# Downsampled probabilities and values as float16 pairs, and one rank per operation, in a fused attention and gated-MLP kernel

## The chip, the cores and the metric

One core of a Trainium2 chip. The metric is device time in microseconds of one execution; lower is better. Engines: PE (TensorE), DVE (VectorE), ACT (ScalarE), POOL (GpSimd), SP (SyncE, which issues most transfers).

## The reference

Attention of 8 batches x 8 heads, 576 positions, 64 numbers a head, feeds a gated MLP. The attention is the sum of two branches: one on queries, keys and values averaged over groups of 4 positions (144 groups), its output repeated 4 times; one on the full positions with a band mask of 3 on either side.

```python
# Attention, per head; sm_attn is softmax(q k^T / 8) v
q_d, k_d, v_d = (a.reshape(B, H, 144, 4, 64).mean(axis=3) for a in (q, k, v))
out_up = np.repeat(sm_attn(q_d, k_d, v_d), 4, axis=2)
out_local = sm_attn(q, k, v) with scores where |i - j| >= 4 set to -1e9
x = (out_up + out_local) as [batch, 576, 512]
# gated MLP
h = np.maximum(x @ w_in, 0.0)
u, v = h[..., :512], h[..., 512:]
v_n = (v - mean(v)) / sqrt(var(v) + 1e-6)
v_s = einsum('ts,bsd->btd', w_spatial, v_n) + b_spatial
out = (u * v_s) @ w_out
```

## The kernel before, in words

**Pieces.** The work is cut into pieces, each an operation of one engine with its inputs, outputs and buffers (`plan.op`). Two heads make a pair, so there are 4 pairs a batch and 32 in all, numbered n. A pair's attention: sums over groups of 4 (`sum1`, `sum2`), banded scores on PE (S, L694, forty f32 matmul records of 64x64; the mask is added by DVE, or by four mask products on PE, L687, for pairs marked T in `ON`), downsampled scores (Sd, L741), softmax steps on DVE, ACT and POOL, f32 transposes of the probabilities on PE (T, L770, banded; Td, L804, downsampled), copies to SBUF by ACT, and two value products on PE (AV, L837, banded; AVd, L827, downsampled). The sum of both goes to `x`; from batch 1 on it is split into an f16 hi part (ACT) and an f16 lo part (DVE, L865).

A batch's gated MLP: V pieces (L899 to L908), U pieces (L965, L970), spatial pieces SP (L992 to L995: 14 matmuls) and output pieces O (L1029: 12 matmuls). Batch 0 uses f32 weights straight away (f32 V and U pieces); from batch 1 on every product is three f16 products, hi x hi, hi x lo, lo x hi. The weights come as 64-bit words which DVE and ACT turn into f32 and then into f16 pairs in the opening (`low`, `shrink`, `body`, `sign`, `whi`, `wlo`; L473 to L488, L446, L449). The scale of each split comes from a bound: a transpose (L416), a maximum (L419), a product with ones (`spread`, L422) and five small DVE steps.

**Td and AVd before.** `normal_d` multiplies the 3 x 144 exponentials in `ed` by the inverse sums, in f32. `turn_d` (L804) transposes them in six f32 products with an identity, 72 keys at a time, into two PSUM banks; ACT copies each (`copy_d`, L808). `values_d` (L827) multiplies them by the downsampled f32 values `tv` in four f32 products: two column halves (heads) times two blocks of 72 keys.

**Order.** Before anything is emitted, `plan.run` (L143 to L244) lists the pieces: for each engine it takes, among those that could start within `NEAR` ns of the first, the one of the smallest rank, with `STAY` off for PE pieces in the array's present mode, and goes by assumed durations. The result is a fixed order in each engine's queue. Ranks are the pair's number plus a number for the kind of piece, from the tables `RANK` (attention), `MRANK` (gated MLP), `WRANK` and `SRANK` (weights). While PE would idle before 110 us of the plan, products on constants are put in (`warm`, L1080). `ON` says which engine does a step for the n-th pair (A ACT, D DVE, P POOL).

Of the kernel before, what the change touches and what calls it, by code (L numbers as in the profile page):

```python
# [76 lines left out]
class Plan:  # L77
# [14 lines left out]
    def buf(self, tag):  # L92
        b = Buf(tag, self.count[tag])
        self.count[tag] += 1
        return b

    def op(self, eng, ns, fn, r=(), w=(), hold=(), after=(), rank=0.0, lag=None, port=False, kb=0, mode="",
           name=""):
# [25 lines left out]
        for t in (*r, *w, *hold):  # L124
            b = t if isinstance(t, Buf) else t[0] if isinstance(t, tuple) else None
            if isinstance(b, Buf) and b not in o.bufs:
                o.bufs.append(b)
                b.left += 1
# [3 lines left out]
    def run(self, near=150.0, stay=0.0, dma=(1500.0, 4.2, 500.0), emit=True):  # L132
# [6 lines left out]
        since = {t: [0.0] * len(v) for t, v in self.places.items()}  # L139
        end = 0.0  # L140
# [108 lines left out]
RANK = {"load": [-94.58, 127.99, 43.89, 60.21, -107.64, 28.27, -122.54, 3.37, -146.09, 126.37],  # L249
        "vload": [183.17, 159.9, -72.4],  # L250
        "vabs": [15.5, 92.34, -30.01],
        "tv": [14.64, -124.04, -101.65],
        "sum": [65.95, 32.66, 176.64, 185.55, 155.19, 82.2, 190.54, 200, 174.16, 200],
# [22 lines left out]
SRANK = {"WV": [-14.84, -71.59, -150.09, -200],
        "WU": [-144.08, 40.42, -170.35, -167.93],
        "WSP": [-187.21, -48.19, -200, -172.6, -159.59],
        "WO": [-94.51, 19.4, -185.76, 42.74]}
NEAR = 101  # L280
STAY = 24.8
# [8 lines left out]
ON = {"shrink": "AAAADA",  # L290
      "sum": "DPDPDPPDPDDDDPDDPD",
      "mask": "DDDTTTDTDTDDDDDDTDDDDTD",
      "norm": "PPPDPPDPDDDPPDDDDPDDPPPPDPPPDP",
      "normd": "DPPPPPDDPPAPPAAPPPPDPDPPDDAPDAD",
      "vlo": "DPDDDPPDPDDDDPDDDPPDPPDDDDPPPDPPDPDDDPD"}
# [3 lines left out]
def tile_kernel(ctx, tc, qk, vw, v4, w_in, wT, bsp, w_out, out, emit=True):  # L299
# [58 lines left out]
    places("g", 2, [P, NF, 2, HA[1]], F16)  # L358
# [4 lines left out]
    places("gt", 1, [P, NF, 2, 2 * TAIL], F16)  # L363
# [5 lines left out]
    places("tv", 2, [72, NP, 4 * D], F32)  # L369
# [9 lines left out]
    places("pdT", 1, [72, 2, 3, 96], F32)  # L379
# [17 lines left out]
    places("wst", NT + 1, [P, S], F32)  # L397
# [200 lines left out]
    x_of, tail_of, tv_of, sx_of, v_of, gt_of, og_of = {}, {}, {}, {}, {}, {}, {}  # L598
# [42 lines left out]
    def attention(n):  # L641
# [484 lines left out]
```

## Time and profile before

| | |
|---|---|
| median of 3 runs | 580.74 us (578.71 to 585.12) |
| profiled execution | 581.14 us |
| its span, first to last instruction | 579.3 us |
| mean granted TensorE clock | 0.979 of full |
| PE busy | 555.9 us |
| DVE, ACT, POOL busy | 427.9, 333.6, 142.0 us |

The span is what the trace covers; the profiled execution is 1.8 us longer. Busy time of PE counts a matmul from its start to its modelled end, so neighbours overlap; the chain of waits counts from start to start.

### The profile page before, as it was taken

Reading aid. Unit: us, or ns where it says so; the run is one execution under the profiler, and the core shown is the slowest. Engines: PE = TensorE matmul, PEld = TensorE weight load, DVE = VectorE, ACT = ScalarE, POOL = GpSimd, SP = SyncE. Lnnn points to the kernel's source line nnn. Section 1 sums busy time; section 2 is a strip of 40 time slices with the busy share of each in tenths; the row PEclk is TensorE's granted clock in tenths of the full one; section 3 lists DMA queues with packets and bytes.
Section 4 is the critical chain, followed back from the end, with each engine's and each line's share of the span. In section 5 each row is a group of like instructions: output and inputs, shape, how many; then the busy total and the mean of one; then the engine's idle time right before and its main releaser. Section 6 shows DMA issues by size and latency. Waiting matters only on the chain.

```text
span 579.3 us, 15196 instructions
## 1 busy us (share of the span) xinstructions
PE 555.9 (96%) x6159; PEld 374.3 (65%) x6159; DVE 427.9 (74%) x1129; ACT 333.6 (58%) x901; POOL 142.0 (25%) x157
## 2 busy tenths in 40 slices
PE   5769899999999999999999999999999999999997
PEld 2456357776677666776668656775777666675573
DVE  6999996985887588884979497888768776636250
ACT  4676676665774568454665476555755555534322
POOL 3533343002422125001610163102511051002100
PEclk9876999999999999999999999999999999999999
DMA  9997634023550344323542145324431101010102
GB/s 266 282 296 219 181 72 125 30 65 108 129 116 1 119 106 107 101 84 103 108 116 70 37 105 124 102 84 105 107 101 61 60 1 40 19 37 0 40 16 91
DMA packets 37386, 56.98 MB, mean 98 GB/s; under 512 B 3651, under 2 KB 24131, under 8 KB 37317
## 3 DMA queue, kind: packets, MB, share of 16 engines
q1 hardware_dynamic: 35012, 48.94, 27.3%
q0 software_dynamic: 2304, 7.08, 7.5%
q8 instruction: 48, 0.79, 0.6%
q14 instruction: 22, 0.17, 0.1%
HBM read 46.57 MB, written 9.44 MB: 97 GB/s over the span
## 4 chain that ended last, share of the span: by engine, by line
PE 84%; DVE 9%; issue 4%; ACT 2%; POOL 1%; ACTq 0%; POOLq 0%; DVEq 0%
PE pmb L1029 5%; PE pmc L992 5%; PE pmb L992 5%; PE pma L903 5%; PE pmd L1029 4%; PE pma L992 4%; PE pmc L970 4%; PE pma L1029 4%; PE pmd L992 3%; PE pmb L970 3%; PE pma L970 3%; PE pmd L903 3%; PE pmc L903 3%; PE pmd L970 3%; PE pmc L1029 2%
## 5 line engine op out<-in xcount | busy, mean ns | idle before, releaser
L992 PEld LDWEIGHTS <-vha 128*128 128x128 f16 x768 | 73.8, 98 | 21.1 <-issue 2.6
L970 PEld LDWEIGHTS <-win 128*128 128x128 f16 x672 | 65.0, 98 | 19.4 <-issue 2.7
L762 POOL TENSOR_TENSOR sa<-sa,sma 128x640 f32<-128x640 f32 x12 | 17.3, 1440 | 110.1 <-DVE sma L729 71.9
L1029 PEld LDWEIGHTS <-gb 128*128 128x128 f16 x192 | 18.6, 98 | 20.4 <-issue 0.2
L1029 PEld LDWEIGHTS <-ga 128*128 128x128 f16 x192 | 18.4, 98 | 20.2 <-issue 0.2
L992 PE MATMUL pmc<-wsp,vha 128*128 128x256 f16 (+1 forms) x216 | 29.2, 284 | 0.0
L992 PE MATMUL pmb<-wsp,vha 128*128 128x256 f16 (+1 forms) x216 | 28.8, 283 | 0.0
L992 PE MATMUL pma<-wsp,vha 128*128 128x320 f16 (+1 forms) x180 | 24.7, 286 | 0.0
L792 POOL TENSOR_TENSOR eda<-eda,smda 128x432 f32<-128x432 f32 x8 | 8.9, 1113 | 60.7 <-DVE smda L783 30.6
L707 DVE TENSOR_TENSOR sa<-paa,mask 128x384 f32<-128x384 f32 (+1 forms) x16 | 7.1, 486 | 21.9 <-PE paa L694 21.9
L992 PE MATMUL pmd<-wsp,vha 128*128 128x320 f16 (+1 forms) x156 | 22.1, 291 | 0.0
L934 POOL TENSOR_TENSOR stc<-stc,mhalf 128x1 f32<-128x1 f32 (+1 forms) x13 | 9.7, 744 | 49.6 <-DVE stc L915 49.6
L762 POOL TENSOR_TENSOR sb<-sb,smb 128x640 f32<-128x640 f32 x7 | 9.9, 1421 | 39.9 <-ACT gb L1002 26.6
L934 POOL TENSOR_TENSOR sta<-sta,mhalf 128x1 f32<-128x1 f32 (+1 forms) x14 | 11.4, 813 | 29.0 <-DVE sta L915 29.0
L934 POOL TENSOR_TENSOR stb<-stb,mhalf 128x1 f32<-128x1 f32 (+1 forms) x13 | 11.6, 894 | 20.9 <-DVE stb L915 20.9
L1029 PE MATMUL pmb<-wo,ga 128*128 128x512 f16 x72 | 16.6, 379 | 0.0
L1029 PE MATMUL pma<-wo,gb 128*128 128x512 f16 x72 | 16.5, 379 | 0.0
L758 ACT ACTIVATE sa<-sa 128x640 f32<-128x640 f32 x16 | 11.8, 739 | 5.7 <-DVE sw L427 3.0
L903 PEld LDWEIGHTS <-xa 128*128 128x128 f16 x84 | 8.2, 98 | 9.9
L610 POOL DMA_DIRECT2D tva<-v_dram x12 | 11.2, 932 | 13.6 <-DMA tva<-v_dram 13.6
L778 ACT ACTIVATE eda<-pmc,mxda 128x144 f32<-128x144 f32 x19 | 7.1, 377 | 11.9 <-DVE mxda L746 10.0
L1029 PE MATMUL pmd<-wo,ga 128*128 128x512 f16 x60 | 13.8, 379 | 0.0
(1034 smaller groups left out, 1692.5 us busy)
## 6 DMA issues: line engine op xcount, KB each, us to landing
qka<-qk_dram SPq DMA_DIRECT2D x16, 576.0 KB, 4.3
qkb<-qk_dram SPq DMA_DIRECT2D x16, 576.0 KB, 5.3
tva<-v_dram POOLq DMA_DIRECT2D x12, 288.0 KB, 4.9
tvb<-v_dram POOLq DMA_DIRECT2D x12, 288.0 KB, 4.4
stg<-w_in_dram SPq DMA_DIRECT2D x5, 512.0 KB, 5.1
out_dram<-rowa SPq DMA_DIRECT2D x8, 256.0 KB, 2.0
out_dram<-rowc SPq DMA_DIRECT2D x7, 256.0 KB, 4.3
more<-w_in_dram SPq DMA_DIRECT2D x3, 512.0 KB
```

What stands on the lines that cost most here:

```text
L610: plan.op("POOL", 850, lambda r=r: nc.gpsimd.dma_start(t.ap, v4[b, r], accum_op=ALU.add), w=[t], rank=rank + 2.0 + 0.3 * r, kb=288, name="tv")
L707: nc.vector.tensor_tensor(sv, pv, mask[:, None, None, :].broadcast_to(list(pv.shape)), op=ALU.add)
L758: exp_of.append(plan.op("ACT", 643, lambda: nc.scalar.activation(s.ap, s.ap, AF.Exp, scale=1.0 / 8.0), w=[s], rank=R["E"], name="exp"))
L762: plan.op(nm, 0, lambda: side(nm).tensor_tensor(s.ap, s.ap, sm.ap[:, :, None].broadcast_to([P, NW, 64]), op=ALU.mult), r=[sm], w=[s], rank ...
L778: nc.scalar.activation(ed.ap[:, a, :], down(a), AF.Exp, bias=mxd.ap[:, a:a + 1], scale=1.0 / 128.0, accum_out=smd.ap[:, a:a + 1])
L792: side(nd).tensor_tensor(ed.ap, ed.ap, smd.ap[:, :, None].broadcast_to([P, 3, G]), op=ALU.mult)
L903: nc.tensor.matmul(ps.ap, xs[c].ap[:, i, t * P:(t + 1) * P], win[:, c, j, FF:], start=(c == 0 and (i, j) == (0, 0)), stop=(c == NC - 1 and ...
L934: plan.op("POOL", 830, lambda: nc.gpsimd.tensor_tensor(st.ap[:r, 8:9], st.ap[:r, 8:9], mhalf[:r], op=ALU.pow), w=[st], rank=rank - EVICT, ...
L970: nc.tensor.matmul(ps.ap[:, :n], win[:, c, i, ft * P:(ft + 1) * P], xs[c].ap[:, j, HA[h]:HA[h + 1]], start=(c == 0 and (i, j) == (0, 0)), ...
L992: nc.tensor.matmul(ps.ap[:, :n], vh.ap[:, c, i, fs], wsp[:, c, j, hs], start=(c == 0 and (i, j) == (0, 0)), stop=False)
L1029: nc.tensor.matmul(ps.ap, g.ap[:, c, i, k:k + P] if t < NT else gt.ap[:, c, i], wo[:, c, j, :], start=(c == 0 and (i, j) == (0, 0)), stop= ...
```

## The change

1. **AVd and Td in f16, from batch 1 on.** The downsampled values `tv` are scaled and split into an f16 hi (ACT) and lo (DVE, L807, two instructions of 512 columns a batch), and four SP transfers (`move`, L813) lay them out as 96 rows of `th`. The normalized probabilities are written as f16 hi into `eh` (`normal_d`), and three new DVE instructions of 144 columns a pair write the lo part (`rest_d`, L978). Nine f16 transposes (L1011) replace six f32 ones and one bank the two; one ACT copy of 864 columns replaces two of 288. Ten f16 products (L1049) replace four f32 ones. The copy of the result (`dn`) is scaled. Batch 0 keeps the f32 forms (now L995 and L1040).
2. **Ranks.** A table `ORDER` gives every operation its rank by its number in the program, and overrides the ranks that the calls pass on. `NEAR` and `STAY` change.
3. **Engines.** `ON` is rewritten: among pairs, masks by PE (T) rise from 7 to 11; some sums, normalizing steps and lo parts change sides, and ACT takes 16 normalizing steps of the downsampled branch where it had 5.
4. **Memory.** First slots of `tv`, `th` and `eh` lie in the staging of the spatial weights `wst`, those of `g` and `gt` in the staging of w_in; `kept` holds them back until that staging is released. Two f16 identities are made by POOL at the start.

```diff
+        o.rank = ORDER[len(self.ops)]
         self.ops.append(o)
...
+ORDER = [
+    37.60, -174.26, -1122.41, -103.57, -12.79, -6.00, -3.24, -1114.52, -2299.76, -1110.97, -18.29, -668.02, -984.84, -2316.33, -1043.76,
...
-NEAR = 101
-STAY = 24.8
+NEAR = 131.8
+STAY = 5.08
...
-      "mask": "DDDTTTDTDTDDDDDDTDDDDTD",
+      "mask": "DDDTTTDTDDTTDTDDDDTTDTDDDDDDTD",
...
+        plan.op("ACT", 1000, lambda: nc.scalar.activation(both(tx, 0), tv.ap.rearrange("p j (k d) -> p j k d", k=2), AF.Copy, scale=sx.ap[:72, 10:11]),
+                r=[tv, sx.sub(10)], w=[tx.sub(0)], rank=rank, name="thi")
+
+        def low():
+            x = tv.ap.rearrange("p j (k d) -> p j k d", k=2)
+            for k in range(2):
+                nc.vector.scalar_tensor_tensor(tx.ap[:, 2 + k], x[:, :, k], sx.ap[:72, 10:11], tx.ap[:, k], op0=ALU.mult, op1=ALU.subtract)
...
+        def spread_rows():
+            a, z = th.ap[:, ::2], tx.ap
+            for dst, src in ((a[:72], z[:, ::2]), (a[72:], z[:24, 1::2]), (th.ap[0:96:2, 1::2], z[24:, 1::2]), (th.ap[1:96:2, 1::2], z[24:, 1::2])):
+                nc.sync.dma_start(dst, src)
...
+        def rest_d():
+            for a in range(3):
+                nc.vector.scalar_tensor_tensor(eh.ap[:, a, :, 1], ed.ap[:, a, :], smd.ap[:, a:a + 1], eh.ap[:, a, :, 0], op0=ALU.mult, op1=ALU.subtract)
...
+        def turn_h():
+            v = turned(ptd[0])[:96, :9 * 112].rearrange("p (c a q) -> p c a q", c=3, a=3)
+            for c in range(3):
+                for a in range(3):
+                    x = eh.ap[:112, a, 96:].rearrange("p k x -> p (k x)") if c == 1 else eh.ap[:112, a, :96, c // 2]
+                    nc.tensor.matmul(v[:, c, a], x, cross16 if a == 2 else ident16, start=True, stop=True, is_transpose=True)
...
+        def values_h():
+            t = half_t().rearrange("p (c a h q) -> p c a h q", c=3, a=3, h=2)
+            w = th_of[b].ap
+            passes = ((0, 0), (2, 0), (0, 2), (1, 1), (1, 3))
+            for i, (c, k) in enumerate(passes):
+                for h in range(2):
+                    nc.tensor.matmul(pw.ap[h * 64:h * 64 + 64, :G], w[:, k, p, h * D:h * D + D], t[:, c, :, h, :],
+                                     start=i == 0, stop=i == len(passes) - 1)
```

What stands on PE ahead of the first spatial piece, before (L687 and L694 banded scores with the mask by PE, L416 and L422 bounds, L804 Td, then L992, the spatial piece):

```order
L694 MATMUL paa<-qkb 64x64 x20
L694 MATMUL pab<-qka 64x64 x20
L416 MATMUL pma<-ident,uta 8x128
L416 MATMUL pmd<-ident,sw 4x128
L804 MATMUL pmb<-ident,eda 72x112 x2
L804 MATMUL pmb<-cross,eda 72x112
L804 MATMUL pmc<-ident,eda 72x112 x2
L804 MATMUL pmc<-cross,eda 72x112
L422 LDWEIGHTS one
L422 MATMUL pma<-uta,one 128x1
```

The same place now, from the banded scores on (L873; L1049 is pair 4's new AVd, ten loads and ten products, of which the last are shown; L575 the product with ones; L1011 the next pair's new Td, its first of nine):

```order
L1049 LDWEIGHTS th_126
L1049 MATMUL pma<-pdTa,th_126 64x144
L1049 LDWEIGHTS th_126
L1049 MATMUL pma<-pdTa,th_126 64x144
L575 LDWEIGHTS one
L575 MATMUL pmc<-uta,one 128x1
L1011 LDWEIGHTS wst
L1011 MATMUL pmb<-ident_86,wst 96x112
```

Pair 4's AVd has moved ahead of the first spatial piece (before, it followed it), and reads `th`, which four SP transfers fill.

DVE at the end of the opening, before (L940 a lo part of V, L473 to L488 conversion of w_out, L918 a normalizing step, L668 group sums, L707 mask, L419 the maximum that opens the spatial pieces):

```order
L940 TENSOR_TENSOR vha<-rowd,vha 128x512
L473 TENSOR_SCALAR mbc<-more 128x512
L473 TENSOR_SCALAR mbd<-stg 128x512
L918 TENSOR_SCALAR rowb<-rowb,stb 64x512
L484 SCALAR_TENSOR_TENSOR mbc<-rowe,mbc 128x512
L484 SCALAR_TENSOR_TENSOR mbd<-rowa,mbd 128x512
L488 SCALAR_TENSOR_TENSOR mbc<-rowe,mbc 128x512
L488 SCALAR_TENSOR_TENSOR mbd<-rowa,mbd 128x512
L668 TENSOR_TENSOR kdb<-suma 128x288
L707 TENSOR_TENSOR sb<-pab,mask 128x2x3x64
L707 TENSOR_TENSOR sb<-pab,mask 128x2x2x64
L419 TENSOR_REDUCE uta<-pma 8x1
```

And now (L807 the new lo part of the downsampled values; L1144, L1166, L847, L886 and L572 are L918, L940, L668, L707 and L419 of before; L961 and L962 the inverse of a sum):

```order
L807 SCALAR_TENSOR_TENSOR txa<-wst,sxa,txa 72x512 x2
L1144 TENSOR_SCALAR rowc<-rowc,stb 64x512
L1166 TENSOR_TENSOR vha<-rowd,vha 128x512
L572 TENSOR_REDUCE sw<-pmd 4x1
L847 TENSOR_TENSOR kdb<-suma 128x288
L961 TENSOR_SCALAR smda<-smda 128x3
L962 RECIPROCAL smda<-smda 128x3
L886 TENSOR_TENSOR sa<-pab,mask 128x2x3x64
L886 TENSOR_TENSOR sa<-pab,mask 128x2x2x64
L572 TENSOR_REDUCE uta<-pmc 8x1
```

The conversions of w_out now stand earlier, and the lo part of the values (L807) lies ahead of the maximum, with eight other instructions between.

## Rows read from the trace of the kernel before

**Rows 1.** The page: span, busy time of each engine with its share, and PE and its granted clock (tenths) in 40 equal slices.

```profile
span 579.3 us, 15196 instructions
PE 555.9 (96%) x6159; PEld 374.3 (65%) x6159; DVE 427.9 (74%) x1129; ACT 333.6 (58%) x901; POOL 142.0 (25%) x157
PE   5769899999999999999999999999999999999997
PEclk9876999999999999999999999999999999999999
```

**Rows 2.** Busy time by stretch: from and to (us), length, then each engine's busy us and instructions, granted clock, DMA share, GB/s.

```profile
0.00:54.00 54.00, 38.58 (x598) 25.73 (x598) 45.77 (x104) 31.94 (x88) 20.79 (x36) 0.81 0.93 270
54.00:70.00 16.00, 13.54 (x44) 5.86 (x44) 15.72 (x37) 10.86 (x26) 4.95 (x6) 1.00 0.72 208
70.00:98.00 28.00, 27.52 (x182) 17.64 (x182) 22.93 (x62) 20.07 (x51) 12.91 (x12) 0.94 0.31 61
98.00:576.00 478.00, 476.22 (x5339) 325.09 (x5338) 343.49 (x929) 270.69 (x737) 103.34 (x104) 1.00 0.28 78
```

**Rows 3.** The chain of waits, start and length in us, counted to the next piece's start.

```profile
95.14 0.26 PE paa L687 x4
95.40 0.58 PE paa L694 x40
...
101.09 0.65 PE pma L827 x8
...
103.38 1.31 PE pma L992 x12
...
106.44 1.63 PE pmd L992 x12
...
113.40 0.29 PE pmc L804 x3
113.69 0.29 PE pmd L804 x3
...
116.16 0.11 PE pma L741 x2
...
575.39 0.69 ACT rowa L1042
```

**Rows 4.** The stretch from 98 to 576 us, first the instructions of L827 alone, then those of L804 alone: PE's busy time and count, then its weight loads.

```profile
98.00:576.00 478.00, 20.10 (x224) 12.59 (x224) 1.00 0.28 78
98.00:576.00 478.00, 20.03 (x162) 16.36 (x162) 1.00 0.28 78
```

**Rows 5.** Weight loads by line: durations in ns (least/median/most), first and last start in us, rows x columns and type. L416, L804, L770 are transposes, L687 the bf16 mask, L694 and L899 ordinary f32 products.

```profile
L416 PEld LDWEIGHTS pmd<-ident,utc x2: 87/87/87, 229.7 to 422.0; 128*8 128x8 f32 x2
L804 PEld LDWEIGHTS pmc<-ident,eda x16: 112/113/116, 15.8 to 388.1; 112*72 112x72 f32 x16
L770 PEld LDWEIGHTS pab<-ident,sb x45: 139/141/142, 26.5 to 422.7; 128*128 128x128 f32 x45
L687 PEld LDWEIGHTS <-mask_a x28: 103/103/125, 31.4 to 331.5; 64*64 64x64 bf16 x28
L694 PEld LDWEIGHTS paa<-qka x320: 129/135/135, 6.1 to 426.2; 64*64 64x64 f32 x160
L899 PEld LDWEIGHTS pmb<-mbb,xb x4: 190/190/190, 54.5 to 62.7; 128*128 128x128 f32 x4
```

**Rows 6.** PE in the opening, in order of time: start, us, line, operation, tiles, shapes, count, and the idle time before it with what ended it. First V piece, a U step, first spatial piece.

```profile
53.99 1.13 PE L899 MATMUL pmb<-mba,xa 128*128 128x512 f32 x2
...
69.86 0.70 PE L965 MATMUL pmc<-xd,mbh 128*128 128x256 f32 x2 [1.78 <-DVE mbh L488]
...
98.06 1.48 PE L992 MATMUL pmb<-wsp,vha 128*128 128x256 f16 x12
```

**Rows 7.** DVE at the end of the opening, in the same form.

```profile
88.39 0.69 DVE L940 TENSOR_TENSOR vha<-rowd,vha 128x512 f16<-128x512 f32 x1 [0.44 <-ACT vha L938]
...
96.64 0.89 DVE L707 TENSOR_TENSOR sb<-pab,mask 128x384 f32<-128x384 f32 x2 [3.66 <-PE pab L694]
97.45 0.27 DVE L419 TENSOR_REDUCE uta<-pma 8x1 bf16<-8x128 f32 x1
```

**Rows 8.** Instructions grouped by line and form, count | busy us, mean ns | idle before; then two rows of transfers: an issue of two on SP in order of time, and a group of stores with KB each and us to landing.

```profile
L665 DVE TENSOR_TENSOR suma<-qka 128x576 f32<-128x576 f32 x14 | 10.7, 761 | 2.0 <-DMA qka<-qk_dram 2.0
L668 DVE TENSOR_TENSOR kda<-suma 128x288 f32<-128x288 f32 x13 | 6.7, 512 | 0.3
L865 DVE SCALAR_TENSOR_TENSOR xf<-xfa,sxa,xf 128x576 f16<-128x576 f32 x4 | 3.1, 784 | 0.0
L449 DVE SCALAR_TENSOR_TENSOR wo<-mba,sw,wo 128x512 f16<-128x512 f32 x1 | 0.7, 743 | 0.0
L808 ACT COPY pdTa<-pmb 72x288 f32<-72x288 f32 x19 | 7.5, 393 | 2.4 <-PE pmb L804 2.4
L792 POOL TENSOR_TENSOR eda<-eda,smda 128x432 f32<-128x432 f32 x8 | 8.9, 1113 | 60.7 <-DVE smda L783 30.6
...
97.54 1.29 SPq L624 DMA_DIRECT2D vd<-vw_dram  x2
...
out_dram<-rowd SPq DMA_DIRECT2D x4, 128.0 KB, 2.2
```

More of the change, by code (lines that the diff above doesn't have):

```diff
@@ L124, in op @@
         for t in (*r, *w, *hold):
+            if isinstance(t, Buf):
+                o.bufs += [x for x in self.held.get(t.tag, ()) if x not in o.bufs]
             b = t if isinstance(t, Buf) else t[0] if isinstance(t, tuple) else None
@@ L127, in op @@
                 o.bufs.append(b)
-                b.left += 1
+        for b in o.bufs:
+            b.left += 1
+        o.rank = ORDER[len(self.ops)]
         self.ops.append(o)
@@ L139, in run @@
         since = {t: [0.0] * len(v) for t, v in self.places.items()}
+        for b in (x for v in self.held.values() for x in v):
+            since[b.tag][b.slot] = None
         end = 0.0
@@ L276 @@
[L276 to L279, printed above, removed]
-NEAR = 101
-STAY = 24.8
+RANK = {"load": [-38.34, -38.34, -38.34, -38.34, 194.73, 194.73, 194.73, 194.73, -104.21, -104.21],
+        "vload": [28.68, 82.28, 98.76],
+        "vabs": [1.11, -27.85, 2.97],
+        "tv": [-60, -3.63, -131.09],
+        "th": [-60, -60, -60],
+        "sum": [-7.7, -7.7, -7.7, -7.7, 83.34, 83.34, 83.34, 83.34, 129.45, 129.45],
[7 rows of a table added]
+        "AVd": [-158.96, -158.96, -158.96, -158.96, -95.27, -95.27, -95.27, -95.27, -2.28, -2.28],
+        "AV": [192.01, 192.01, 192.01, 192.01, -47.84, -47.84, -47.84, -47.84, 10.31, 10.31],
+        "X": [-69.34, -69.34, -69.34, -69.34, -39.39, -39.39, -39.39, -39.39, 64.63, 64.63]}
@@ L800, in turn_d @@
+        ptd, pdT = [plan.buf("pm") for _ in range(2 if whole else 1)], plan.buf("pdT")
+        KEYS = (72, 72)
         def turn_d():
-            for kc in range(2):
-                v = ptd[kc].ap[:72, :384].rearrange("p (a q) -> p a q", a=3)
+            for kc, n in enumerate(KEYS):
+                v = ptd[kc].ap[:n, :384].rearrange("p (a q) -> p a q", a=3)
                 for a in range(3):
-                    nc.tensor.matmul(v[:, a, :112], ed.ap[:112, a, kc * 72:kc * 72 + 72], cross if a == 2 else ident[:112, :112],
+                    nc.tensor.matmul(v[:, a, :112], ed.ap[:112, a, kc * 72:kc * 72 + n], cross if a == 2 else ident[:112, :112],
@@ new lines, in half_t, with copy_h @@
+        def half_t():
+            return pdT.ap.rearrange("p c a q -> p (c a q)").bitcast(F16)[:, :9 * 96]
+        def copy_h():
+            nc.scalar.copy(half_t().rearrange("p (c q) -> p c q", q=96),
+                           turned(ptd[0])[:96, :9 * 112].rearrange("p (c q) -> p c q", q=112)[:, :, :96])
+        copies = [copied]
+        if whole:
+            plan.op("PE", 560, turn_d, r=[ed], w=list(ptd), hold=[pdT], rank=R["Td"], lag=PEL, mode="F", name="Td")
+            for kc in range(2):
+                copies += [plan.op("ACT", 290, lambda kc=kc: copy_d(kc), r=[ptd[kc]], w=[pdT.sub(kc)], rank=R["Td"] - EVICT, name="copyTd")]
+        else:
+            plan.op("PE", 442, turn_h, r=[eh.sub(0), eh.sub(1)], w=list(ptd), hold=[pdT], rank=R["Td"], lag=PEL, mode="F", name="Td")
+            copies += [plan.op("ACT", 790, copy_h, r=list(ptd), w=[pdT.sub(0), pdT.sub(1)], rank=R["Td"] - EVICT, name="copyTd")]
```

129 lines of the change are left out of this document (84 added, 45 removed), and 134 rows, old and new, of tables (ORDER, RANK).

## The prediction

> **What bounds the kernel now.** Read the page's busy times first: PE is busy 96% of the span, no other engine over 74% [rows 1]. A busy PE need not be a bound, so the table of stretches comes next [rows 2]. It splits the run in two. From 98 us to 576 us PE is busy for all but 1.8 us of 478, at full granted clock (1.00, the level of 2.4 GHz). Of that 1.8, 0.7 is the last copy, after PE has finished [rows 3], so PE really waits 1.1 us. Before 98 us it is another program: PE idles for 18.4 us, the clock is 0.81 of full up to 54 us, and DVE is busy 45.8 of 54 and then 15.7 of 16 us [rows 2]. So the opening belongs to loads and DVE, and from the first spatial piece, at 98.06 us [rows 6], every nanosecond that PE needs is a nanosecond of span. Third, the chain of waits prices the pieces from start to start, which the modelled ends of matmuls don't [rows 3].
>
> **Values matmul of the downsampled branch (AVd, L827).** On the chain four f32 products, recorded as eight matmuls, take 0.65 us [rows 3]. After 98 us there are 224 records, 28 pieces [rows 4]. A 64x144 f32 round with two column halves side by side takes 0.11 on the chain (L741, [rows 3]), so four rounds are 0.45 to 0.49 and first load and drain the other 0.16. For f16 I use two spatial pieces: twelve 256-column matmuls take 1.31 and twelve of 320 take 1.63, so 109 and 136 ns, 0.42 ns a column [rows 3]. 144 columns are 62 ns. The new piece has ten f16 products in five such rounds: 0.31 + 0.16 = 0.47, an estimate. One of the 28 now stands ahead of the first spatial piece, so 28 x 0.65 - 27 x 0.47 = 18.2 - 12.7 = 5.5 us go. Bounds: if the two halves don't run side by side, ten rounds are 0.62 + 0.16 = 0.78 and 27 of them cost 2.9 us more than before; if the drain shrinks too, 0.36 and 8.5 us go.
>
> **Transposes (Td, L804).** Six f32 transposes take 0.29 + 0.29 us [rows 3]; 162 records, 27 pieces, are left after 98 us [rows 4]: 15.7. Now nine f16 ones of 112 columns. Streaming costs 49 ns each by the same slope. But each loads 96 columns of weights first, and the trace has no f16 load of 96. The nearest rows: f32 loads in transposes last 87 ns for 8 columns, 113 for 72, 141 for 128, that is 0.45 ns a column; the bf16 mask's 64 columns last 103 [rows 5]. By that slope 96 columns take 43 ns of throughput, under the 49, and the load hides. Nine are 0.445; the order has 26 after the first spatial piece: 11.6, so 4.1 go. The other end: f32 loads of ordinary products last 135 ns for 64 columns and 190 for 128, 0.86 a column [rows 5]; 96 columns would be 83 ns and bind, 0.74 a piece, 26 x 0.74 = 19.2, a loss of 3.5. I take the first, because a transpose is what it is. The Trainium skill, "TensorE: Matmul & The Clock Gate", section "LDWEIGHTS (loading the stationary operand)", speaks against the change here: the load takes columns divided by 1.2 GHz, so 80 ns for 96; by it, an estimate, a piece is 0.72 and the term turns from -4.1 to +3.0. Its slope of 0.83 is the one of the ordinary f32 rows; the transposes' rows [rows 5] contradict it.
>
> **What else moves on PE.** Mask products by PE rise from 7 to 11 pairs, all four after 98 us: 4 x 0.26 = 1.0 [rows 3]. One downsampled score piece moves ahead: three rounds, 0.3. All other pieces (V, U, SP, O, S, T, AV) stand in the same numbers on both sides of the first spatial piece. Sum after it: -5.5 - 4.1 + 1.0 - 0.3 = -8.9 us.
>
> **The opening.** Two things reach the first spatial piece later. (a) DVE: ahead of the reduction that opens the spatial pieces (L419, 97.45 us) the order now has more. Six residue instructions of 144 columns are new to the trace: bounded by 0.1 and by the 576-column form's 0.78, I estimate 0.25, 1.5 in all; two low halves of the values of 512 columns at 0.74, 1.5; one more pair sum, 0.76 + 0.5; eight small ones, 1.2 [rows 7, 8]. That is 5.5 us, against 3.66 + 0.44 us of DVE idle time there [rows 7], which they fill: 1.4 later. (b) A new path: the low halves, then four SP transfers, then pair 4's values matmul, which stands on PE ahead of the spread, a Td and the first spatial piece; all three queue behind it. On DVE 2.8 us of work lie between the low halves and the reduction, so they end at 96.0; four issues at 0.65 are 2.6, landing 2.2 more by a 128 KB store [rows 8]: 100.8 at the latest, 99 if issues overlap flight. Then 0.47 + 0.1 + 0.45: the first spatial piece at 100 to 101.8, 2 to 3.7 late. For the other sign: four V pieces now stand ahead of the first U piece where three did, and PE's 1.8 us wait for the last converted weight (69.86, [rows 6]) can go. I take +2.5, the lower part of (b), bounds -1.8 to +8 (the opening's own clock, 0.81, shows what PE idle there does).
>
> **Edits costed at nothing.** After 98 us DVE gets 26 x 0.75 of residues and a few low halves, about 25 us on 343 busy of 478 [rows 2]; ACT's copy of the transposes is one of 864 columns instead of two of 288, at 393 ns each [rows 8], about 0.2 more, and more of the normalizing stands on ACT. PE's own work covers both. Its margin is the distance in PE's order from a pair's scores to its transposes: never under 6.4 us of PE work now, once 4.5, mostly 6.3 and up before; the chain between (maxima, exponential, inverse, normalizing up to 1.1 on POOL [rows 8], and now a residue of 0.75) grows by that last step. I allow 0.5 us, bounds 0 to 20 (all residues shown). POOL's normalizing now writes f16 at a stride; POOL is idle enough [rows 2]. The last five O pieces and the final copy and store are unchanged.
>
> **Sum.** The profiled execution took 581.1 us (span 579.3 and 1.8 around it). 581.1 - 8.9 + 2.5 + 0.5 = 575.2. It stood 0.4 above the median of 580.74, so the forecast is 574.8, 1.0% under; about 1% is what a measurement of this kernel can tell from none.
>
> **Rivals.**
> 1. *Weight loads bind the f16 transposes.* For it: the ordinary f32 slope; against it: the transposes' slope, both in [rows 5]. Term +3.5 instead of -4.1: 582.4. The skill's section on loads is this rival's rule. A second rule of that page ("Wait — 56ns, not 53.3ns?") gives some 62 ns of sequencer time per matmul, an estimate of 0.78 for the ten products; here forty matmul records of L694 take 0.58 us [rows 3], 15 ns each, so it doesn't bind.
> 2. *The opening eats it.* The transfers land late, PE idles into the lower clock: +8 instead of +2.5, 580.3. For it: 0.81 before 54 us [rows 2].
> 3. *Slower: the residue is late in every pair.* Place: PE in front of each f16 transpose; price: the whole new DVE step, 0.75 us, 28 times, +21 instead of +0.5: 595. It decides for slower from 12 us, 0.43 us a pair. For it: a strict order, and DVE at 80% and over of the 54 to 98 us. Against: PE lost only 1.1 us after 98 us before with the same distances.
> 4. *The opening gains.* The wait at 69.86 goes and the transfers find cover: -1.8 instead of +2.5 and no stall, 570.0.
>
> **How the numbers follow.** Forecast (572 to 577.5): 0.42, of which 0.25 lies over 1% below the median; rival 4: 0.23; rival 2: 0.12; rival 1: 0.12; rival 3: 0.11. Faster by over 1%: 0.25 + 0.23 = 0.48. Slower: 0.11 and the tail of rival 1, 0.12. Within: 0.40. Range 568.5 to 585: from 1.5 under rival 4 to 2.6 over rival 1; rival 3 and the tails stay out.
>
> **What would show it.** Right: L1011's nine transposes 0.44 to 0.46 us on the chain; L1049's ten products 0.45 to 0.5; the first L1218 at 100 to 102 us; PE waiting under 2 us after it. Wrong: L1011 spaced at 80 ns (rival 1); the first L1218 after 105 or before 98 (rivals 2, 4); PE waits at L1011 on DVE L978 of 0.4 us a pair (rival 3).

## The result and the profile after

The changed kernel took 571.78 us (median, 570.31 to 572.09) against 580.24 before: 0.984 of it, 95% interval 0.9803 to 0.9878. Two later groups of runs gave 0.9819 (0.9793 to 0.9844) and 0.9813 (0.9786 to 0.9841). So the change gains 1.6 to 1.9%, 9 to 11 us. The forecast was 574.8, a gain of 5.9; the measured median lies 0.2 us under the band that the prediction called its forecast (572 to 577.5), and inside its range.

The page, with the lines that answer to [rows 1]:

```profile
span 570.3 us, 15614 instructions
PE 547.1 (96%) x6307; PEld 368.4 (65%) x6307; DVE 449.1 (79%) x1227; ACT 358.5 (63%) x913; POOL 139.0 (24%) x162
PE   5778799999999999999999999999999999999997
PEclk9758999999999999999999999999999999999999
```

PE has 148 instructions more and 8.8 us less to do; DVE has 21 us more. PE's share of the span is the same 96%, so the bound has not moved: the program is shorter by what PE does less. The table of stretches, columns as in [rows 2], with the last stretch ending 0.6 us after PE does (before, 0.7):

```profile
0.00:54.00 54.00, 39.48 (x601) 26.35 (x602) 44.71 (x109) 34.88 (x94) 20.30 (x42) 0.78 1.00 262
54.00:70.00 16.00, 12.41 (x48) 5.77 (x46) 15.59 (x42) 11.31 (x28) 5.83 (x7) 1.00 0.88 207
70.00:98.00 28.00, 27.99 (x189) 17.70 (x185) 25.56 (x69) 21.39 (x58) 7.42 (x8) 0.94 0.41 86
98.00:567.00 469.00, 467.18 (x5479) 318.62 (x5474) 363.27 (x1012) 290.71 (x737) 105.42 (x107) 1.00 0.31 84
```

The opening is as it was: PE idles for 18.1 us of the first 98 (18.4 before), and the granted clock is 0.78 up to 54 us where it was 0.81. After it PE is busy for all but 1.8 us, though DVE now has 77% of that stretch where it had 72%. The chain of waits around the first spatial piece, and its end, as in [rows 3]:

```profile
95.98 2.42 DMA th<-txa
...
98.54 0.32 PE pma L1049 x4
98.96 0.58 PE pmb L1011 x9
99.53 1.31 PE pmd L1218 x12
...
107.57 0.43 PE pmb L1049 x10
...
114.56 0.45 PE pma L1011 x9
...
566.47 0.69 ACT rowa L1268
```

The chain starts a piece at the modelled end of the one before it; by its own start the first spatial piece comes at 99.37, and that is the time used below. L1049 (new AVd) takes 0.43 us on the chain, L1011 (new Td) 0.45. The path of the low halves is on the chain, as forecast: the transfer of `th`, the rest of pair 4's AVd, a Td, the first spatial piece. In the opening itself, as in [rows 6], the waits have changed places:

```profile
68.76 0.77 PE L949 MATMUL paa<-ident,sb 128*128 128x128 f32 x5 [3.59 <-POOL sb L941]
...
70.09 2.07 PE L1125 MATMUL pmb<-mba,xa 128*128 128x512 f32 x2
...
98.54 0.32 PE L1049 MATMUL pma<-pdTa,th 96*64 96x144 f16 x4 [0.41 <-DMA th<-txa]
```

The wait of 1.78 us for the converted weights is gone, a wait of 3.59 for POOL's normalizing stands just ahead of it, and after it a V round takes 2.07 us where the rounds before took 1.02: PE is on its lower level. It was on it at that place before, too; over 70 to 98 us the granted clock is 0.94 in both kernels. PE waits 0.41 us for the transfer. After the first spatial piece the groups of waits name two of any size (us in total, times, longest):

```profile
PE pma L1011 <- DVE eh L978: 0.4, 1, 0.4
PE pma L569 <- ACT ug L1202: 0.3, 1, 0.3
```

**Where the time came from.** I give each PE instruction the time from its start to the next one's start, and sum by kind, from the first spatial piece (L992, now L1218) to the start of PE's last instruction. These sums hold the waits, and add up to the whole stretch. The remaining kinds (spatial, O, V, T, S, AV, spreads) differ by 0.2 us at most.

| kind | before | after | difference | forecast |
|---|---|---|---|---|
| AVd | 18.20 | 11.76 | -6.4 | -5.5 |
| Td, with the waits within and right behind it | 15.82 | 13.15 | -2.7 | -4.1 |
| mask by PE | 0.48 | 1.12 | +0.6 | +1.0 |
| Sd | 10.25 | 9.73 | -0.5 | -0.3 |
| U, with a wait of 0.7 us at 288 us before | 84.14 | 83.25 | -0.9 | part of +0.5 |
| whole stretch | 476.86 | 466.64 | -10.2 | -8.4 |
| first spatial piece at | 98.06 | 99.37 | +1.3 | +2.5 |

### The profile page after: what moved, and what is told of

Read it like the earlier page. It is cut to its first block, busy times and chain, and to the rows that moved or that the text cites. A ratio compares the mean times of both kernels' runs of the same rounds, so it can differ in the third digit from the quotient of the medians.

```text
span 570.3 us, 15614 instructions
## 1 busy us (share of the span) xinstructions
PE 547.1 (96%) x6307; PEld 368.4 (65%) x6307; DVE 449.1 (79%) x1227; ACT 358.5 (63%) x913; POOL 139.0 (24%) x162
## 4 chain that ended last, share of the span: by engine, by line
PE 82%; DVE 10%; DMA 4%; ACT 2%; issue 1%; SPq 0%; POOL 0%; DVEq 0%; POOLq 0%; ACTq 0%
PE pma L1255 5%; PE pmc L1255 5%; PE pmd L1218 4%; PE pma L1196 4%; PE pma L1218 4%; PE pmb L1218 4%; PE pmc L1218 4%; PE pmb L1196 4%; PE pma L1129 4%; PE pmc L1129 4%; PE pmd L1255 3%; PE pmb L1255 3%; PE pmd L1129 3%; PE pmb L1129 3%; PE pmd L1196 3%; PE paa L1060 2%
## 5 line engine op out<-in xcount | busy, mean ns | idle before, releaser
L1218 PEld LDWEIGHTS <-vha 128*128 128x128 f16 x768 | 73.6, 98 | 19.5
L1196 PEld LDWEIGHTS <-win 128*128 128x128 f16 x672 | 64.8, 98 | 18.4
L1255 PEld LDWEIGHTS <-more 128*128 128x128 f16 x192 | 18.5, 98 | 20.8
L1255 PEld LDWEIGHTS <-g 128*128 128x128 f16 x192 | 18.3, 98 | 20.8
L1218 PE MATMUL pmd<-wsp,vha 128*128 128x320 f16 (+1 forms) x192 | 27.5, 292 | 0.0
L1218 PE MATMUL pma<-wsp,vha 128*128 128x256 f16 (+1 forms) x192 | 26.2, 286 | 0.0
L1218 PE MATMUL pmb<-wsp,vha 128*128 128x256 f16 (+1 forms) x192 | 25.5, 282 | 0.0
L1218 PE MATMUL pmc<-wsp,vha 128*128 128x256 f16 (+1 forms) x192 | 25.5, 282 | 0.0
L1255 PE MATMUL pmc<-wo,g 128*128 128x512 f16 x72 | 16.5, 379 | 0.0
L978 DVE SCALAR_TENSOR_TENSOR eh<-eda,smda,eh 128x144 f16<-128x144 f32 x42 | 15.8, 440 | 0.1
L763 POOL DMA_DIRECT2D tv<-v_dram x12 | 11.5, 955 | 16.4 <-DMA tv<-v_dram 16.4
L904 DVE TENSOR_REDUCE smb<-sb 128x10 f32<-128x640 f32 x16 | 12.9, 809 | 1.3 <-ACT sb L937 1.3
L937 ACT ACTIVATE sb<-sb 128x640 f32<-128x640 f32 x16 | 11.8, 735 | 3.3 <-DVE sb L901 3.1
L1255 PE MATMUL pma<-wo,more 128*128 128x512 f16 x60 | 13.8, 379 | 0.0
L1255 PE MATMUL pmc<-wo,more 128*128 128x512 f16 x60 | 13.8, 379 | 0.0
```

What stands on the lines that cost most here:

```text
L763: plan.op("POOL", 850, lambda r=r: nc.gpsimd.dma_start(t.ap, v4[b, r], accum_op=ALU.add), w=[t], rank=rank + 2.0 + 0.3 * r, kb=288, name="tv")
L904: nc.vector.tensor_reduce(sm.ap, s.ap, axis=AX.X, op=ALU.add)
L937: exp_of.append(plan.op("ACT", 643, lambda: nc.scalar.activation(s.ap, s.ap, AF.Exp, scale=1.0 / 8.0), w=[s], rank=R["E"], name="exp"))
L978: nc.vector.scalar_tensor_tensor(eh.ap[:, a, :, 1], ed.ap[:, a, :], smd.ap[:, a:a + 1], eh.ap[:, a, :, 0], op0=ALU.mult, op1=ALU.subtract)
L1196: nc.tensor.matmul(ps.ap[:, :n], win[:, c, i, ft * P:(ft + 1) * P], xs[c].ap[:, j, HA[h]:HA[h + 1]], start=(c == 0 and (i, j) == (0, 0)), ...
L1218: nc.tensor.matmul(ps.ap[:, :n], vh.ap[:, c, i, fs], wsp[:, c, j, hs], start=(c == 0 and (i, j) == (0, 0)), stop=False)
```

## The experiments

Each ratio is to the kernel before, run on the same chip. "First" is the start of the first spatial piece, "rest" from there to the start of PE's last instruction, "idle" PE's idle time in the rest, all from the one profiled execution of each. The residue is the lo part of the probabilities (`rest_d`), the halves are the hi and lo parts of the downsampled values. The second run of the changed kernel shared its chip with f16 from batch 2, old ranks and masks on DVE, the third with f16 from pair 6; the other kernels are set against 0.9824, the mean of its three ratios.

| kernel | us | ratio, 95% interval | first | rest | idle |
|---|---|---|---|---|---|
| changed | 571.78 | 0.984 (0.9803 to 0.9878) | 99.37 | 466.64 | 0.8 |
| changed, again | 570.26 | 0.9819 (0.9793 to 0.9844) | 97.30 | 466.57 | 0.8 |
| changed, third | 570.73 | 0.9813 (0.9786 to 0.9841) | 97.08 | 466.66 | 0.8 |
| f32, two banks | 584.46 | 1.0049 (1.0018 to 1.0079) | 94.93 | 482.79 | 5.2 |
| f32, one bank | 579.49 | 0.9958 (0.9934 to 0.9982) | 94.33 | 478.16 | 2.4 |
| residue twice | 583.24 | 1.0018 (0.9992 to 1.0044) | 98.95 | 478.36 | 6.5 |
| no residue | 569.53 | 0.9806 (0.9756 to 0.9857) | 95.90 | 466.59 | 1.0 |
| extra transposes | 584.20 | 1.0036 (1.0013 to 1.0059) | 97.92 | 480.47 | 0.4 |
| f16 from batch 2 | 571.44 | 0.9821 (0.98 to 0.9843) | 94.78 | 470.56 | 2.2 |
| f16 from pair 6 | 569.53 | 0.9783 (0.9756 to 0.981) | 92.91 | 469.17 | 1.1 |
| old ranks | 626.40 | 1.0776 (1.075 to 1.0803) | 107.28 | 510.34 | 30.5 |
| masks on DVE | 578.17 | 0.9942 (0.9921 to 0.9963) | 99.50 | 475.21 | 8.9 |

**The same kernel again, twice**, without an edit, as a measure for the rest.

> The changed kernel once more, beside the others of this group on the same chip, so that they can be compared with it directly: 0.984 of the kernel before.

> The changed kernel once more, beside the next one on the same chip: 0.982 to 0.984 of the kernel before; first spatial piece between 97 and 99.5 us, 466.6 us from its start to PE's last instruction.

The rest of the run agrees within 0.1 us in three profiles, taken on at least two chips; the first spatial piece moves by 2.3 us (97.08 to 99.37). So a rest is comparable to a tenth of a microsecond, a "first" only to two, and the single "first" of before, 98.06, lies within what the changed kernel shows.

**f32 under the new ranks, two kernels.** The first undoes the f16 path and keeps ranks and masks:

```diff
-  plan.op("DVE", 790, rest_d, ...)          # likewise halves, thi, low, spread_rows
+  plan.op("DVE", 790, lambda: None, ...)
-  ptd = [plan.buf("pm") for _ in range(2 if whole else 1)]
+  ptd = [plan.buf("pm") for _ in range(2)]
-  plan.op("PE", 442, turn_h, ...)     plan.op("PE", ..., values_h, ...)
+  plan.op("PE", 442, turn_d, ...)     plan.op("PE", ..., values_d, ...)
```

> The changed kernel with its own ranks, but the downsampled path of every batch in f32 as before: six f32 transposes into two PSUM banks, four f32 value products; no residue, no low halves, no transfers of them. Theory (the arithmetic on PE makes the gain, the ranks only keep PE fed): a transposing piece goes back from 0.444 to 0.576 us and a value piece from 0.435 to 0.65, so 26 x 0.13 + 27 x 0.215 = +9.2 us against the changed kernel, 0.4 off for the wait for the transfers, 581, and PE waits of under 2 us after the first spatial piece. Rival A (the new ranks make the gain): the pieces are longer, but the time stays under 576. Rival B (the second PSUM bank that f32 transposes take is what costs): pieces as in the theory and PE waits on top, over 585.

The second puts both halves of the transposes into one bank:

```diff
+  ptd = [plan.buf("pm") for _ in range(2 if whole else 1)]
+  v = ptd[kc if whole else 0].ap...
```

> As the kernel with f32 in every batch, but from batch 1 on the second half of the transposes is written over the first in one bank (so half of the transposed probabilities is lost); the transposes, copies and products are as many and as long. Theory: 581, as with two banks. Rival A: under 576. Rival B (the bank costs): 579 to 582 here, and 3 us or more over it with two banks.

Measured: 584.46 and 579.49, that is 0.022 and 0.013 of the time before above the changed kernel, 13 and 8 us. With one bank the rest is 11.5 us longer: AVd 17.55 us instead of 11.76 (5.8), Td 15.49 instead of 12.47 of work (3.0), idle 1.6 more, one Sd piece more behind the first spatial piece (0.7). The first spatial piece comes 2 to 5 us earlier: there are no low halves to wait for, and fewer pieces stand ahead of it. Rival A falls, neither is under 576. Rival B holds beside the theory, though two banks stay just under its 585 and PE waits more than the theory's 2 us: the second bank costs another 5 us (0.9%), of which the rest shows 4.6 (2.8 of it idle, 0.6 a Td piece more behind the first spatial piece). That nine f16 transposes fit into one bank is a gain, under these ranks, that I had no term for.

**Residue twice.** `rest_d` runs over (0, 1, 2, 0, 1, 2).

> The changed kernel with the residue of the probabilities computed twice in a row (six instead of three DVE instructions of 0.31 us, 0.93 us a pair, 26 us of DVE in all). In the changed kernel's trace the residue ends between 0.17 and 5 us before its transposes in 24 of the 26 pairs after the first spatial piece, under 0.93 us before in ten. Theory (the residue is hidden by what is left of that margin): each pair pays 0.93 less its margin and no more, 4.8 us in all, 576.6; PE waits in front of the transposes in those ten pairs. Rival A (DVE has room, the order adapts): under 573. Rival B (the residue was late in every pair and DVE's queue drags on): 0.93 x 26 = 24 us, 590 or more.

Measured: 583.24, 0.019 over the changed kernel, 11 us; the rest 11.7 longer. The groups of waits after the first spatial piece, the three largest (us in total, times, longest):

```profile
PE paa L949 <- POOL sb L941: 1.3, 2, 0.9
PE pma L569 <- ACT ug L1202: 1.2, 1, 1.2
PE pma L1011 <- DVE eh L978: 0.9, 1, 0.9
```

And two stretches of 5 us, columns as in [rows 2]:

```profile
165.00:170.00 5.00, 3.54 (x24) 2.46 (x24) 3.50 (x14) 2.90 (x7) 2.27 (x2) 0.83 0.40 61
170.00:175.00 5.00, 5.00 (x121) 3.94 (x119) 3.29 (x9) 1.67 (x8) 0.00 (x0) 0.83 0.36 114
```

Both theories of the extremes fall: it is not free, and not 24 us. Mine was half the size. It counted the wait in front of the transposes (4.8); the transposes with the waits within and right behind them take 6.7 more (19.87 us instead of 13.15). And it left out two things. What DVE does next is late too (probabilities, U's bounds). And after one wait of 1.17 us and the next, 0.26, the clock was down. PE in order of time there:

```profile
166.60 0.27 PE L569 MATMUL pma<-ident,utb 128*8 128x128 f32 x1 [1.17 <-ACT ug L1202]
167.14 0.77 PE L949 MATMUL paa<-ident,sa 128*128 128x128 f32 x5 [0.26 <-DVE sa L941]
...
167.94 2.43 PE L1218 MATMUL pmb<-wsp,vha 128*128 128x256 f16 x12
```

The same twelve matmuls take 1.48 us at full clock [rows 6]. A mean of 0.83 over 10 us is another 1.7 us, more than the two waits just before it. It is the one place behind the first spatial piece where this run's clock was down, though a wait of 0.94 and others of 0.9 stand elsewhere in it.

**No residue.** The place in the order is kept, the three instructions are left out (what is transposed as residue is what the buffer held; POOL sets one of the two buffers to zero at the start):

```diff
-  plan.op("DVE", 790, rest_d, ...)
+  plan.op("DVE", 790, lambda: None, ...)
```

> The changed kernel without the residue of the probabilities (the three DVE instructions a pair, 26 us of DVE; what is transposed as residue is whatever the buffer held), everything else in the same order. Theory (the residue is hidden but for the waits in front of transposes that the changed kernel's trace shows, 0.4 + 0.6 us): from the first spatial piece to PE's last instruction 465.5 to 466.0 us against 466.6, the time within 2 us of the changed kernel. Rival (DVE's queue as a whole is late by what the residue takes): 463 us or less, 3 us or more under it.

The rest is 466.59 against 466.64: behind the first spatial piece the residue costs nothing that shows. The theory had 465.5 to 466.0: Td's waits go (its sum is 12.39 us instead of 13.15), and another wait takes their place, 0.5 us for POOL's normalizing:

```profile
PE paa L950 <- POOL sb L942: 0.5, 1, 0.5
PE pma L570 <- ACT ug L1203: 0.3, 1, 0.3
```

So in the rest one residue is worth 0 and a second one 11.7 us. The changed kernel stands just ahead of the point where DVE decides. The first spatial piece comes at 95.90, 1.2 us ahead of the earliest of the changed kernel's three; with one profile of this version, that is a hint and no more.

**Extra transposes**, nine more ahead of each nine, in four shapes:

```diff
+  w, m = ((96, 112), (96, 48), (48, 112), (48, 48))[n % 4]
+  ...matmul(v[:w, c, a, :m], x[:m, :w], ident16[:m, :m], is_transpose=True)
```

> The changed kernel with nine more f16 transposes ahead of the nine of each pair, written over by them, in four kinds by pair: 96 loaded columns and 112 moved, 96 and 48, 48 and 112, 48 and 48. Seven pairs of each. Theory (the larger of load at 0.45 ns a column and stream at 0.42 decides, and every ns of PE is a ns of span): spacings of 49, 43, 49 and 22 ns, seven times 0.44 + 0.39 + 0.44 + 0.20 = 10.3 us, 582 to 583. Rival A (load takes 0.83 ns a column): 80, 80, 49 and 40 ns. Rival B (a fixed time of 49 ns each): 49 in all four, 12.3 us, 584. Rival C (PE has room beside the longest chain): the spacings of the theory, but under 577.

The chain of waits, L1012 the extra nine, one pair of each shape (loaded by moved columns) in the order 48 by 112, 48 by 48, 96 by 112, 96 by 48:

```profile
113.05 0.55 PE pma L1012 x9
...
120.27 0.33 PE pmc L1012 x9
...
136.07 0.44 PE pma L1012 x9
...
149.46 0.52 PE pmd L1012 x9
```

Read them with care: the real nine behind them are 96 by 112, and where the extra ones have another shape, the last of them lasts 84 to 94 ns longer than the others, and the first of the real nine 89 instead of 54. Within a piece the starts of the records are 49, 25, 49 and 45 ns apart (medians). So a load of 96 columns passes in 45 ns and one of 48 in 25 at most (its 48 moved columns may be what binds); taken at 25, that is 0.42 ns a column and 5 over; 112 moved columns take 49. Rival A (0.83 a column) and rival B (a fixed time) fall. The Trainium skill, "TensorE: Matmul & The Clock Gate", section "LDWEIGHTS (loading the stationary operand)", has columns divided by 1.2 GHz, 80 and 40 ns here: the runs show 45 and 25. The real transposes are bound by their stream, with 4 ns to spare before the load binds. And rival C falls: 12.5 us of extra transposes (10.3 in the theory, which had nothing for the changes of shape) made the rest 13.8 longer and the time 12: PE's time is the span's time.

**f16 from batch 2 on** (`plain_d = b < 2` chooses the f32 path, and the halves of batch 1 are left out of the order).

> The changed kernel with the f16 path from batch 2 on; batch 1 keeps the f32 path (two banks for its transposes), without residue, low halves and their transfers. In the kernel with f32 in all batches the first spatial piece began at 94.3 us, in the changed one at 99.4. Theory (the low halves and transfers of batch 1, on DVE and SP, and the pieces of its first pairs make these 5 us): the first spatial piece at 94 to 96 us, four pairs pay 4 x (0.215 + 0.13) = 1.4 us on PE and up to 1 for banks, 2.5 to 3.5 us under the changed kernel. Rival (other pieces that the ranks put ahead make them): the first spatial piece stays at 98 to 99.5, 1.4 to 2.4 us over the changed kernel.

The first spatial piece came at 94.78, as the theory had it, but the rest grew by 4.0 us instead of 1.4 to 2.4 (Td 1.6 more work, since one piece that stood ahead of the first spatial piece is now behind it, AVd 0.7, and 1.4 more idle), and the time is the changed kernel's: neither theory nor rival had that. The opening was not 5 us to be had: beside the changed kernel of the same chip (97.30) it is 2.5.

**f16 from pair 6 on** (`plain_d = n < NP + 2`, and the halves' steps of batch 1 with a rank of at least 75).

> The changed kernel with f32 for the downsampled path of pairs 4 and 5 alone, the two whose pieces stand ahead of the first spatial piece, and the halves of batch 1's values and their transfers ranked behind it. Theory (what reaches the first spatial piece later is the halves and the transfers of batch 1; with f16 from batch 2 on it began at 94.8 us, against 97.3 and 99.4): the first spatial piece at 94.5 to 95.5 us, two pairs pay 2 x (0.215 + 0.13) = 0.7 us and moved pieces 0.5 more, so 1 to 3 us under the changed kernel. Rival (what is saved in the opening comes back as waits of DVE and PE behind it, as with f16 from batch 2 on, where 4.0 us came back): within 1 us of it.

First 92.91, rest 469.17: 4.2 us earlier and 2.5 longer than the changed kernel beside it, and 569.53 against 570.73 us, 0.2% under it. The intervals overlap (0.9756 to 0.981, 0.9786 to 0.9841), so that this version is the faster one is what its trace says, and the times don't settle it. It does not show that the transfers were the brake either: under these ranks they left earlier, at 87.3 us instead of 93.3, not later.

**Old ranks by kind**, those of the kernel before for pairs and pieces:

```diff
-  o.rank = ORDER[len(self.ops)]
-  RANK, MRANK, NEAR, STAY of the changed kernel
+  RANK, MRANK, NEAR, STAY of the kernel before
```

> The changed kernel with the ranks by kind of piece that the kernel before had for pairs and pieces (those of the weights are the changed kernel's own by kind, and the steps of the values' halves have -60). Theory (the f16 products make the gain on PE, one rank for every operation only keeps the longer chain to the transposes covered): pieces on PE as in the changed kernel (0.444 and 0.435 us), waits of PE of 5 us or more after the first spatial piece, most in front of the transposes, and a time of 578 or more. Rival (the ranks don't matter, DVE has room): 571 to 575.

The weights' ranks, the choice of engines (`ON`) and the places in memory stay the changed kernel's. Measured: 626.4 us, 7.8% over the kernel before. AVd is longer by 0.7 (one more piece stands behind the first spatial piece), Td's work by 3.0; PE is idle for 30.5 us of the rest, and the clock is 0.97 over 100 to 560 us. The largest groups of waits:

```profile
PE paa L948 <- DVE sb L940: 5.3, 5, 1.6
PE pmb L1010 <- ACT eh L971: 4.7, 1, 4.7
PE pmc L1254 <- DVE ug L1234: 2.8, 1, 2.8
```

The rival (the ranks don't matter) falls. In my theory the place was wrong: the new transposes have a quarter of the idle time (7.3 us), those of the probabilities as much (7.5), U's pieces 5.4.

**Masks on DVE** for all pairs from 8 on (the string of masks ends in D only).

> The changed kernel with the mask of all pairs from 8 on added by DVE, none by PE. PE has 28 products less, 1.1 us; DVE has 0.86 us more in each of seven pairs. Theory (the margin in front of the transposes and of the probabilities is 0.2 to 2 us, so what is added to the chain of scores shows): 1 to 5 us over the changed kernel. Rival (PE alone counts after the first spatial piece): 1 us under it.

578.17, 0.012 over the changed kernel, 7 us: PE has 1.1 us less and waits 8.1 more. The rival falls, and the theory's 5 us at most were too few.

```profile
PE pmc L575 <- DVE utb L572: 1.5, 1, 1.5
PE pab L949 <- DVE sa L941: 1.5, 2, 0.8
PE pmd L1196 <- DVE rowd L1156: 1.3, 1, 1.3
```

The clock stayed at 1.00 through all of them. One stretch of 5 us, columns as in [rows 2], with waits of 0.44 and 1.14 us in it:

```profile
292.00:297.00 5.00, 3.43 (x61) 2.28 (x62) 4.82 (x20) 3.46 (x6) 2.41 (x2) 1.00 0.18 62
```

PE is idle there for 1.57 us of 5, more than the 1.46 of the kernel with the residue twice, where the clock fell.

## Why the prediction was right, point by point

**What bounds the kernel: right.** After the first spatial piece a microsecond of PE was a microsecond of the run: upwards by the extra transposes (+12.5 of work, +12 of time), downwards by the change itself (the rest 10.2 shorter, the time 9 to 11).

**AVd: right, a little under-sized.** -5.5 forecast, -6.4 measured. The rounds start 62 to 63 ns apart behind the first (62 forecast from the f16 slope of 0.42 ns a column) and the two halves of a round 3 ns apart, so the halves do run side by side; first load and drain are 0.13 instead of 0.16, and the piece is 0.436 instead of 0.47, 27 times. The Trainium skill, "TensorE: Matmul & The Clock Gate", section "Wait — 56ns, not 53.3ns?", gives its 62 ns a matmul for hardware decode switched off, a condition that the prediction left out beside rival 1. Ten products in 0.436 us are 44 ns each here, so that rule did not bind.

**Td: right in price, off by what stands around it.** 0.444 us a piece in 19 of 26, 0.445 forecast. The view of one line's instructions has the loads of the new kind, to be laid beside those of [rows 5], and the residue (durations least/median/most in ns):

```profile
L1011 PEld LDWEIGHTS <-eh x126: 119/123/127, 96.1 to 483.5; 112*96 112x96 f16 x126
L978 DVE SCALAR_TENSOR_TENSOR eh<-eda,smda,eh x42: 318/375/1382, 56.5 to 481.0; 128x144 f16<-128x144 f32 x42
```

123 ns lie on the transposes' slope (113 for 72 columns, 141 for 128), far from the ordinary f32 one. That slope was the right one of the two; rival 1 (weight loads bind) is refuted twice, by the spacing of 49 ns here and by the 45 for the load alone. What the term missed is 1.6 us in and behind seven pieces: waits of 0.7 at 292 us and 0.4 at 163, 0.15 at 121 (mostly a wait of the next piece), and 0.04 to 0.10 in four, which are no waits. These four stand next to a piece of another tile shape, the banded values (64 rows by 64 columns) or the product with ones (4 or 8 loaded rows), and the transpose at that end takes 143 to 145 ns to the next start instead of 49, or 89 instead of 54, as at the changes of shape in the run with extra transposes. Such an end, PE in order of time:

```profile
436.10 0.26 PE L1011 MATMUL pmb<-ident,wst 112*96 112x112 f16 x2
436.19 0.21 PE L1011 MATMUL pmb<-cross,wst 112*96 112x112 f16 x1
436.34 0.17 PE L575 MATMUL pma<-sxa,one 4*128 4x1 bf16 x1
```

**Masks: over-sized, and the view too narrow.** I had +1.0 for PE (0.6 measured): the 0.26 a mask is a row of the opening, behind it one takes 0.16. And I had nothing on the other side. With all seven masks of the rest given to DVE, the four new ones and the three that the kernel before had there, PE loses 7 us to waits, in front of the banded transposes, U's pieces and the products with ones, none in front of the downsampled transposes. So masks by PE relieve DVE for the whole chain of scores; what the four new ones are worth alone was not tested.

**Edits costed at nothing: the sum was right, the reason was not.** The residue takes 0.93 us a pair (0.28 from one start to the next, 0.375 each; 0.75 forecast for three) and PE lost nothing by it behind the first spatial piece, which the kernel without it shows. But I had argued with a distance of 6.4 us of PE work. The trace after has the residue ending 0.2 to 5 us ahead of its transposes in 24 of 26 pairs, nine of them under 0.93, 9 us ahead in one, and in one 0.8 us after the piece began. This is that pair, DVE, then POOL, then PE:

```profile
290.10 0.63 DVE L974 TENSOR_TENSOR eh<-eda,smda 128x432 f16<-128x432 f32 x1
...
290.95 1.88 DVE L978 SCALAR_TENSOR_TENSOR eh<-eda,smda,eh 128x144 f16<-128x144 f32 x3
...
291.21 1.45 POOL L941 TENSOR_TENSOR sa<-sa,sma 128x640 f32<-128x640 f32 x1 [1.79 <-DVE sma L908]
...
292.21 0.26 PE L1011 MATMUL pma<-ident,eh 112*96 112x112 f16 x2
292.89 0.25 PE L1011 MATMUL pma<-cross,eh 112*96 112x112 f16 x1 [0.41 <-DVE eh L978]
```

The first three transposes read hi alone, the next three both parts; five run, and the sixth waits for the third instruction of the residue. That one lasts 1.38 us instead of 0.375: it began while POOL's product was running and ended 0.17 us behind it. The same holds in two other pairs (at 447.4 and 479.6 us, 1.38 and 1.23 us), whose transposes had the margin for it. So the one residue that came late was late by what it lost beside POOL: at its usual 0.93 us it would have ended 0.2 us ahead of its transposes. Rival 3 (the residue is late in every pair) was one more residue away from half its price.

**The opening: the mechanism was there, the size was not.** I took +2.5 for the low halves, their transfers and the pair's AVd. The path is on the chain and PE waits for it in the place that I named, but earlier. DVE, and SP's issues, with the rows that answer to [rows 7]:

```profile
92.51 1.40 DVE L807 SCALAR_TENSOR_TENSOR txa<-wst,sxa,txa 72x512 f16<-72x512 f32 x2
...
95.40 0.28 DVE L572 TENSOR_REDUCE sw<-pmd 4x1 bf16<-4x128 f32 x1 [0.43 <-PE pmd L569]
...
98.00 0.27 DVE L572 TENSOR_REDUCE uta<-pmc 8x1 bf16<-8x128 f32 x1
...
93.28 3.30 SPq L813 DMA_DIRECT2D th<-txa  x4
```

The low halves ended at 93.9, where I had 96.0: 4.1 us lie between them and the maximum, not 2.8, and the maximum came 0.55 later than before, not 1.4. From the end of the low halves to the last landing, at 98.40, it was 4.5 us (4.8 forecast for the latest). So the price of the path was right and its start was wrong by two microseconds. The sum of the opening is -1.0 to +1.3 in three profiles against the one of before: nothing that can be told apart. By the prediction's own signs, 100 to 102 us was right and under 98 wrong; the three came at 99.37, 97.30 and 97.08. For rival 4 (the opening gains), the wait at 69.86 went as it said; against it, another of 3.59 us came just ahead. This is the term that was mis-sized: 2.5 us of the forecast that the runs don't show.

**The sum.** -8.4 forecast for the rest, -10.2 measured; +2.5 for the opening, -0.1 measured as the mean of three (97.9 against 98.06). So the forecast of -5.9 became -8.5 to -11, near rival 4 (570.0), inside the range of 568.5 to 585. The signs of the terms on PE's pieces were right; the opening's was not, nor that of the 0.5 allowed for new waits (PE's idle time in the rest went from 1.1 to 0.8, and a wait of 0.7 in front of U went). Part of the agreement is luck: AVd gave 0.9 more than forecast and Td 1.4 less.

**What was not foreseen at all** is how much the two halves of the change need each other. f32 with the new ranks is at 1.005 of the time before, f16 with the old ranks at 1.078, both together at 0.982. Both tables of ranks fit one path only, so these are not the prices of the parts by themselves; what is shown is that neither of these two combinations gains. (With one bank, and half of the transposed probabilities lost, f32 under the new ranks is at 0.996.) The new choice of engines and the new places in memory were in both, and apart from the masks no run takes them back, so their share stays open.

## What to carry to other kernels

Where one engine is busy for all of a stretch, price an edit on it by starts on the chain and by the nearest rows of the same kind: the transposes' own loads said rightly that the load hides, and the price of a new piece came to 0.445 us for 0.444; ordinary products' loads would have made it 0.74. Price what goes to the covering engine by the margin that is left afterwards, per pair, not by its busy share: DVE at 77% hid 0.93 us a pair at no cost and could not hide another. When operations are reordered along with a change in arithmetic, test each under the other's order before giving either the credit, and profile the same kernel more than once before explaining a difference of 2 us in its opening.

## What the runs showed of the hardware that was not expected

- A short wait cost more than itself in one place and not in others. With the residue twice, after waits of 1.17 and 0.26 us, with PE idle for 1.46 us of 5, the granted clock was 0.83 over 10 us where the changed kernel has 1.00, and twelve matmuls took 2.43 us instead of 1.48. With the masks on DVE, waits of 0.44 and 1.14 us (idle 1.57 of 5) and a single one of 1.5 left it at 1.00, as did one of 1.4 with f32 in two banks. What made the difference is not shown.
- A DVE instruction of the residue that began while POOL multiplied 128x640 f32 numbers took 1.23 to 1.38 us instead of 0.375, and ended 0.17 to 0.18 us behind POOL's, in all three places of the changed kernel's trace where that happened; its two repeats show the same (1.22 to 1.38).
- f16 transposes pass at 25 ns with 48 loaded and 48 moved columns, 45 with 96 loaded and 48 moved, 49 with 112 moved; at a change of tile shape between two groups of them the last one lasts 84 to 94 ns longer, about twice what one of them takes, and the first of the next 89 instead of 54.
- Three executions of one program, on at least two chips, differ by 2.3 us in the first 98 us and by 0.1 us in the remaining 467.
